# One maximum over two PSUM banks, and one sum for base and running counts, in an attention and mixture-of-experts kernel

## Chip, cores and metric

The kernel runs on one core of a Trainium2 chip. The metric is device microseconds of one execution, the median of three runs. Lower is better.

## The reference

Two stages, the second on the output of the first.

```python
def _attn_ref(q, k, v, omega):            # 8 x 8 heads, 576 tokens, head_dim 64, 128 features
    ...
    def phi(x):
        proj = np.einsum('bhsd,md->bhsm', x, omega)
        sq = np.sum(x * x, axis=-1, keepdims=True) / 2.0
        h = proj - sq
        h = h - np.max(h, axis=-1, keepdims=True)
        return np.exp(h) / np.sqrt(m)
    q_p, k_p = (phi(q_s), phi(k_s))
    kv = np.einsum('bhsm,bhsd->bhmd', k_p, v)
    z = np.sum(k_p, axis=2)
    num = np.einsum('bhsm,bhmd->bhsd', q_p, kv)
    den = np.einsum('bhsm,bhm->bhs', q_p, z)[..., None] + 1e-06
    return num / den
def _moe_ref(x, expert_emb, tau, w1, w2): # 4608 tokens of 512, 8 experts, hidden 1024
    ...                                   # logits of the normalised token and embeddings, one expert each
    out[mask] = gate_w[mask, None] * (np.maximum(x[mask] @ w1[e], 0.0) @ w2[e])
```

Only `proj` and the row maxima and exponentials of it matter here, and the running count of tokens per expert, from which each token's row in a sorted list follows.

## The kernel before

The first phase is attention and routing. It is a loop over steps `i` from 0 to 42. A step takes one tile of 128 tokens of the keys (`k`, tile `i`) and one tile of the queries (`q`, tile `iq = i - 6`); each tile comes in two halves `a` of four heads. So steps 0 to 5 have keys alone, steps 6 to 35 both, and steps 36 to 42 queries alone or nothing but their remainder. The instructions of all engines stand in the order in which the loop writes them out, and each engine takes its own in that order.

In a step with both, `proj` makes two pairs of projections, each four heads times 128 features in one PSUM bank: first `one`, that is `k` half 1 and `q` half 0 (tag `px`), then `two`, that is `k` half 0 and `q` half 1 (tag `py`). The order of the step is:

- TensorE: `proj(one)`; `qtr`, the transposes of the query features of the step before, into the two banks of `nub`; `proj(two)`; in some steps `kv_turn` (below); `num`, the numerators, into `nub`; in some steps `kv_logits`; `kvmm`, the products of key features and values.
- VectorE: maxima of `k` half 1 (L331); a copy of one bank of transposes (L405); maxima of `q` half 0, then of `q` half 1; in some steps `kv_turned` (L376); maxima of `k` half 0; the four operations of `num_out` (L429, L430, L432, L435), which divide the numerators; then what routing has due at the step's end.
- ScalarE: a copy of the other bank of transposes (L405); then the exponentials (`feats`, L338, four to a tile) of `k` half 1, `q` half 0, `q` half 1 and `k` half 0. An exponential takes its row maxima as bias, so it follows them.

Eight times, when a block of keys is complete, `kv_closed` copies its sums on ScalarE, GpSimd regroups them (L363), and in the step after that TensorE turns them (`kv_turn`, L372), VectorE copies the result out of PSUM (`kv_turned`, L376), and TensorE multiplies that copy with the embeddings (`kv_logits`, L384), which writes into one of the banks of `nub`. From step 6 on `kv_turned` stands in the list `then`, which the loop works off after the maxima of `q` half 1 and before those of `k` half 0; for the first block, in step 6, it stands in `after`, ahead of the maxima of `q` half 1. Of the eight steps six have both tiles: 10, 15, 19, 24, 28 and 33. Step 37 has queries alone.

Every three tiles `routed` works through one group: logits, the chosen expert, TensorE's counts `pr` in a bank of `nub` (L473, L475), and at the end of a later step the sum of counts and running counts `run` into `base` (L481) and the update of `run` (L482). GpSimd makes the row numbers from `base` (L484) and writes the tokens to their rows with an indirect DMA.

The second phase goes through 38 blocks of 128 sorted tokens of one expert each, with TensorE full of products with the experts' weights (L241). `bank` gives it PSUM banks by tag, `py` among them.

Of the kernel before, what the change touches and what calls it, by code (L numbers as in the profile page):

```python
# [11 lines left out]
F32 = mybir.dt.float32  # L12
# [5 lines left out]
ALU = mybir.AluOpType  # L18
AX = mybir.AxisListType
ET = mybir.EngineType  # L20
PSUM = bass.MemoryType.PSUM

P = 128
B, H, S, D, M = 8, 8, 576, 64, 128
E, F = 8, 1024
# [5 lines left out]
G = 3  # L31
REG = N + P
# [23 lines left out]
def attention_moe(ctx: ExitStack, tc: tile.TileContext, qT, kT, v1, omT, emb, tau, w1q, w2q, xs, out):  # L56
    nc = tc.nc
# [6 lines left out]
    ps = ctx.enter_context(tc.tile_pool(name="ps", bufs=1, space=PSUM))  # L64
# [214 lines left out]
    with ExitStack() as c1:  # L279
        p1 = c1.enter_context(tc.tile_pool(name="p1", bufs=2))  # L280
        small = c1.enter_context(tc.tile_pool(name="small", bufs=2))
        once = c1.enter_context(tc.tile_pool(name="once", bufs=1))
        nub = c1.enter_context(tc.tile_pool(name="psn", bufs=1, space=PSUM)).tile([P, 2, 512], F32, name="nub")
        nu = [nub[:, a, :] for a in range(2)]


        kva, kvs, st = {}, {}, {}
        sels = [once.tile([P, G + 1, E], BF16, name=f"sel{j}") for j in range(2)]
        for z in sels:
            nc.vector.memset(z, 0.0)  # L290
# [28 lines left out]


        def proj(*which):
            for w, i, a, tag in which:
                st["pj" + w, i, a] = ps.tile([P, 4, M], F32, name=f"pj{w}{i}_{a}", tag=tag, bufs=2)
            for c in range(4):
                for w, i, a, _ in which:
                    r = slice(a * D, (a + 1) * D)
                    nc.tensor.matmul(st["pj" + w, i, a][:, c, :], st[w, i][r, c, :], om[r, :], start=True, stop=True)  # L327

        def maxima(which, i, a, *_):
            nm = small.tile([P, 4], F32, name=f"nm{which}{i}_{a}", tag=f"nm{which}", bufs=4)  # L330
            nc.vector.tensor_reduce(nm, st["pj" + which, i, a], axis=AX.X, op=ALU.max, negate=True)  # L331
            st["nm" + which, i, a] = nm

        def feats(which, i, a, *_):
            pj, nm = st["pj" + which, i, a], st["nm" + which, i, a]
# [103 lines left out]
        def routed(g):  # L439

            eng = nc.gpsimd if g < NTILE // G - 1 else nc.vector

            def total(out, x, axes):

                if eng is nc.vector:
                    eng.tensor_reduce(out, x.rearrange(axes), axis=AX.X, op=ALU.add)
                    return
                for n in (4, 2, 1):
                    eng.tensor_tensor(x[:, :, 0:n] if n > 1 else out.unsqueeze(2), x[:, :, 0:n], x[:, :, n : 2 * n], op=ALU.add)

            bc = lambda a: a.unsqueeze(2).to_broadcast([P, G, E])
            ibc = lambda a: a.unsqueeze(1).to_broadcast([P, G, E])
            new = lambda n, shape, dt=F32: small.tile(shape, dt, name=f"{n}{g}", tag=n)
            raw = new("raw", [P, G, E])
            total(raw, st["lg", g], "p g h e -> p g e h")
            if eng is nc.gpsimd:
                yield
            mx = new("mx", [P, G])
            nc.vector.tensor_reduce(mx, raw, axis=AX.X, op=ALU.max)
            nc.vector.tensor_tensor(raw, raw, bc(mx), op=ALU.subtract)  # L460
            for j in range(G):
                nc.gpsimd.tensor_copy(st["xr", g * G + j][:, DM : DM + E], raw[:, j])
            yield
            sel = sels[g % 2][:, 0:G]
            nc.vector.scalar_tensor_tensor(sel, raw, 0.0, ibc(iotm), op0=ALU.is_ge, op1=ALU.mult)
            nc.vector.tensor_reduce(mx, sel, axis=AX.X, op=ALU.min)
            nc.vector.tensor_tensor(sel, ibc(iotm), bc(mx), op=ALU.is_equal)
            yield

            w = 512 - 8 * E  # L470
            pr = nu[1][:, w - (G + 1) * E : w].rearrange("p (j e) -> p j e", e=E)
            for o in range(0, P, 64):
                nc.tensor.matmul(pr[o : o + 64], tri[:, o : o + 64], sels[g % 2], start=True, stop=False)  # L473
                for j in range(G):
                    nc.tensor.matmul(  # L475
                        pr[o : o + 64, j + 1 :], one16[:, o : o + 64], sel[:, j : j + 1].to_broadcast([P, G - j, E]),
                        start=False, stop=j == G - 1,
                    )
            yield
            base = new("base", [P, G, E])  # L480
            nc.vector.tensor_tensor(base, pr[:, 0:G], run.unsqueeze(1).to_broadcast([P, G, E]), op=ALU.add)  # L481
            nc.vector.tensor_tensor(run, run, pr[:, G], op=ALU.add)  # L482
            yield
            eng.tensor_tensor(base, base, sel, op=ALU.mult)  # L484
            pos = new("pos", [P, G])
            total(pos, base, "p g e -> p g e")
            if g == GPICK:
                pick_first()

            for j in range(G):  # L490
                if j:
                    yield
                posi = new(f"posi{j}", [P, 1], I32)
                eng.tensor_copy(posi, pos[:, j : j + 1])
                xr = st["xr", g * G + j]
                w = nc.gpsimd.indirect_dma_start(
                    out=xs, out_offset=bass.IndirectOffsetOnAxis(ap=posi, axis=0),
                    in_=xr, in_offset=None, bounds_check=ROWS - 1, oob_is_err=False,
                )
                written(w)  # L500
            if g == GPICK:
                early.append(len(put))

        def pick_first():

            cnt = small.tile([P, E], F32, name="cnt0", tag="cnt")
            nc.vector.scalar_tensor_tensor(cnt, iote, -float(REG), run, op0=ALU.mult, op1=ALU.add)
            m = small.tile([P, 1], F32, name="m0", tag="m0")
            nc.vector.tensor_reduce(m, cnt, axis=AX.X, op=ALU.max)
            nc.vector.tensor_scalar(cnt, cnt, m, None, op0=ALU.is_ge)  # L510
            nc.vector.tensor_tensor(cnt, cnt, iotm, op=ALU.mult)
            nc.vector.tensor_reduce(m, cnt, axis=AX.X, op=ALU.min)
            at(ends, st["now"] + 1).append((first_known, m))
# [86 lines left out]
                loadk(i + 1, nc.sync)  # L600
            loadv(i)
        nc.vector.tensor_scalar(om, om, SCALE, None, op0=ALU.mult)  # L602
        warm = ps.tile([P, 512], F32, name="warm", tag="py", bufs=2)
        for j in range(WARM):
            nc.tensor.matmul(warm[:, j % 4 * P : (j % 4 + 1) * P], one16, one16, start=True, stop=True)

# [45 lines left out]
        for i in range(END + 1):  # L652
# [40 lines left out]
            if ts:  # L693
                num(iq - 1)
            go(after, i)
            for p in two[1:]:
                maxima(*p)
            u = (i - 1) % TPS
            sums = [(j, a, b) for j, b in ([(i - 2, 1)] if u == 5 else []) + [(i - 1, int(u > 4))] for a in range(2)] if ss else []
# [4 lines left out]
            go(then, i)  # L704
            for p in one[1:] if two else ():
                feats(*p)
            if one:
                for p in two[:1]:
                    maxima(*p)
            for x in sums:  # L710
                kvmm(*x)
            closed = ss and u in (4, 8)
# [33 lines left out]
            pass  # L746


        vt = nc.vector
        room, at0 = p1.tile([P, 4, P], F32, name="room", tag="kt").rearrange("p c m -> p (c m)"), [0]  # L750

        def t(n, w=E, dt=F32):
# [94 lines left out]
    ring = xgp + [p2.tile([P, PAY], F32, name=f"xg{t}", bufs=1) for t in range(NPRE + 1, 6)]  # L847

    def bank(name, tag, bufs=1):
        return ps.tile([P, 512], F32, name=name, tag=tag, bufs=bufs)  # L850

    def x_of(t, row):
        return xload(t, row, ring[t % len(ring) if t != "x" else 0])
# [330 lines left out]
```

## Time and profile before

| | |
|---|---|
| median of 3 runs | 664.64 us (664.15 to 665.15) |
| profiled execution | 658.2 us, its span from first to last instruction 656.4 us |
| first phase, steps with both tiles | 18.8 us to 184 us of the span |
| busy in the span | TensorE 631.7 us (96%), VectorE 497.3 us (76%), ScalarE 416.9 us (64%), GpSimd 328.5 us (50%) |
| granted TensorE clock | 0.996 of full speed |

The median lies 6.4 us above the profiled execution's own time, and that lies 1.8 us above its span. Busy shares are means over two phases with different limits, and matmuls overlap one another, so a busy TensorE is not a TensorE at its peak.

### The profile page before, as it was taken

The page shows a single profiled execution, that of the slowest core. Times are in us where ns is not written, and L with a number is a line of the kernel's source. Part 1 is how long each engine was busy: PE and PEld are TensorE (multiplying, and loading weights), DVE is VectorE, ACT ScalarE, POOL GpSimd, SP SyncE. Part 2 cuts the span into 40 slices and gives each one's busy share as a digit, 9 for nine tenths or more (in the row PEclk, how much of TensorE's full clock was granted, in tenths as well). Part 3 has the DMA queues.
Part 4 walks back from the last instruction along what each step waited for, and adds up shares of the span by engine and source line. Part 5 has one row for each costly group of instructions (what it writes and reads, how often), then busy time and mean ns, then how long its engine had stood idle before and what let it go on. Part 6 is the DMA issues. An engine that isn't in the chain of part 4 may idle for free. (4 is left out here: it accounts for less than half of the span.)

```text
span 656.4 us, 18641 instructions
## 1 busy us (share of the span) xinstructions
PE 631.7 (96%) x6339; PEld 532.1 (81%) x6340; DVE 497.3 (76%) x952; ACT 416.9 (64%) x1074; POOL 328.5 (50%) x414
## 2 busy tenths in 40 slices
PE   8999999998889999999999999999999999999993
PEld 7899999988877787888788888888888888888872
DVE  4789888899888736778787777777768787777771
ACT  6899899899877236645656565656555656565430
POOL 2013443448885425474556364646455554646352
PEclk9999999999999999999999999999999999999998
DMA  7547667678832388588898888978697878887710
GB/s 252 177 148 228 196 202 212 214 243 285 261 125 97 118 308 259 156 237 198 237 211 223 208 227 190 240 193 232 178 244 184 236 192 196 225 208 212 187 64 34
DMA packets 142362, 131.89 MB, mean 201 GB/s; under 512 B 106742, under 2 KB 106870, under 8 KB 142272
## 3 DMA queue, kind: packets, MB, share of 16 engines
q1 hardware_dynamic: 135808, 110.04, 62.8%
q0 software_dynamic: 6320, 20.38, 7.9%
q8 instruction: 57, 0.93, 0.6%
q10 hardware_dynamic: 144, 0.26, 0.2%
q14 instruction: 33, 0.27, 0.1%
HBM read 83.78 MB, written 21.97 MB: 161 GB/s over the span
## 5 line engine op out<-in xcount | busy, mean ns | idle before, releaser
L241 PE MATMUL nu<-w2h,hl 128*128 (+1 forms) x288 | 113.9, 395 | 0.4 <-DVE hl L948 0.4
L241 PE MATMUL nu<-w2h,hh 128*128 (+1 forms) x288 | 113.9, 396 | 0.0
L241 PE MATMUL nu<-w2l,hh 128*128 (+1 forms) x288 | 113.8, 395 | 0.0
L241 PE MATMUL pa<-w1h,xl 128*128 (+1 forms) x280 | 110.8, 396 | 0.4 <-DVE xl L947 0.4
L241 PE MATMUL pa<-w1h,xh 128*128 (+1 forms) x280 | 111.1, 397 | 0.0
L241 PE MATMUL pa<-w1l,xh 128*128 (+1 forms) x280 | 110.6, 395 | 0.0
L909 ACT ACTIVATE pl<-pa 128x512 uint16<-128x512 uint16 x68 | 40.1, 594 | 94.2 <-PE pa L241 56.0
L905 DVE TENSOR_REDUCE wd<-t 128x1024 uint16<-128x1024 uint16 x68 | 90.0, 1325 | 1.7 <-DMA t<-pl 1.7
L338 ACT ACTIVATE ftk<-pjk,nmk 128x128 f32<-128x128 f32 x288 | 84.9, 427 | 6.3 <-DVE nmk L331 6.0
L207 POOL TENSOR_TENSOR w1l<-raww,w1h 128x1024 f32 x34 | 83.7, 2461 | 7.4 <-DVE w1h L206 5.5
L905 DVE TENSOR_REDUCE pl<-pa 128x512 uint16<-128x512 uint16 x68 | 46.6, 688 | 51.6 <-ACT pl L909 51.5
L338 ACT ACTIVATE ftq<-pjq,nmq 128x128 f32<-128x128 f32 x288 | 80.0, 430 | 8.7 <-DVE nmq L331 7.8
L207 POOL TENSOR_TENSOR w2l<-raww,w2h 128x1024 f32 x34 | 82.1, 2415 | 2.4 <-issue 2.4
L327 PE MATMUL pjq<-om,qt 64*128 64x128 f32 x576 | 75.6, 283 | 1.1 <-ACT ftk L338 0.7
L327 PE MATMUL pjk<-om,kt 64*128 64x128 f32 x576 | 76.3, 285 | 0.3 <-DVE om L602 0.3
L944 ACT ACTIVATE hh<-wd 128x1024 fp32r<-128x1024 f32 x34 | 36.1, 1062 | 60.2 <-DVE wd L905 54.3
L327 PEld LDWEIGHTS pjk<-om,kt 64*128 64x128 f32 x576 | 65.1, 190 | 2.9 <-DVE om L602 0.6
L271 POOL DMA_INDIRECT y<-xgp x20 | 22.7, 1136 | 87.6 <-DVE xgp L248 84.1
L241 PEld LDWEIGHTS nu<-w2h,hl 128*128 128x128 f32 x288 | 54.0, 188 | 13.9 <-DVE hl L948 0.8
L327 PEld LDWEIGHTS pjq<-om,qt 64*128 64x128 f32 x576 | 63.9, 188 | 1.6 <-ACT ftk L338 0.9
L241 PEld LDWEIGHTS nu<-w2l,hh 128*128 128x128 f32 x288 | 54.1, 188 | 13.1
L241 PEld LDWEIGHTS nu<-w2h,hh 128*128 128x128 f32 x288 | 54.1, 188 | 13.0
(311 smaller groups left out, 1270.0 us busy)
## 6 DMA issues: line engine op xcount, KB each, us to landing
raww<-w1q SPq DMA_DIRECT2D x38, 512.0 KB, 3.9
raww<-w2q SPq DMA_DIRECT2D x38, 512.0 KB, 5.2
qt<-qT SPq DMA_DIRECT2D x36, 256.0 KB, 4.3
kt<-kT SPq DMA_DIRECT2D x35, 256.0 KB, 3.0
xgp<-xs SPq DMA_DIRECT2D x20, 260.5 KB, 2.8
xg<-xs SPq DMA_DIRECT2D x18, 260.5 KB, 2.9
rf<-w1q SPq DMA_DIRECT2D x4, 512.0 KB, 5.6
rf<-w2q SPq DMA_DIRECT2D x4, 512.0 KB
```

What stands on the lines that cost most here:

```text
L207: il = nc.gpsimd.tensor_tensor(at(l, dp), raw, at(h, dp).bitcast(F32), op=ALU.subtract)
L241: done.append(nc.tensor.matmul(dst, x[:, c * P : (c + 1) * P], ws.rearrange("p o f -> p (o f)"), start=(begin and i == 0 and k == 0), stop ...
L271: w = nc.gpsimd.indirect_dma_start(out=out, out_offset=bass.IndirectOffsetOnAxis(ap=xg[:, PAY - 1 : PAY].bitcast(I32), axis=0), in_=xg[:, ...
L327: nc.tensor.matmul(st["pj" + w, i, a][:, c, :], st[w, i][r, c, :], om[r, :], start=True, stop=True)
L338: nc.scalar.activation(ft[:, h, :], pj[:, h, :], AF.Exp, bias=nm[:, h : h + 1])
L905: nc.vector.tensor_reduce(to, src.unsqueeze(2), axis=AX.X, op=ALU.max)
L909: nc.scalar.activation(planes[1][:, o : o + 512], halved(src)[:, :, 1], AF.Copy)
L944: nc.scalar.activation(hh, wd[:, 0:F], AF.Relu)
```

## The change

In steps with both tiles the pair `two` goes into one tile of two PSUM banks, and one `tensor_reduce` of 1024 elements per partition (`maxima2`) takes the maxima of both halves, at the place where those of `q` half 1 stood. The maxima of `k` half 0 no longer have an instruction of their own behind `then`. The tag `py` moves from the pool `ps` with two buffers of a bank into the pool `psn` with one buffer of two banks; the warm-up tile goes to `px`; the second phase takes `py` from its own pool.

In `routed` one addition of 32 elements gives `base` and the new running counts together, where there were an addition of 24 elements and one of 8.

```diff
-        nub = c1.enter_context(tc.tile_pool(name="psn", bufs=1, space=PSUM)).tile([P, 2, 512], F32, name="nub")
+        psn = c1.enter_context(tc.tile_pool(name="psn", bufs=1, space=PSUM))
+        nub = psn.tile([P, 2, 512], F32, name="nub")
...
-        kva, kvs, st = {}, {}, {}
+        kva, kvs, st = {}, {}, {"run": run}
...
         def proj(*which):
-            for w, i, a, tag in which:
-                st["pj" + w, i, a] = ps.tile([P, 4, M], F32, name=f"pj{w}{i}_{a}", tag=tag, bufs=2)
+            if which and which[0][3] == "py":
+                two = psn.tile([P, 2, 4, M], F32, name=f"pj{which[0][1]}_2", tag="py")
+                for j, (w, i, a, _) in enumerate(which):
+                    st["pj" + w, i, a], st["two", w, i, a] = two[:, j], two
+            else:
+                for w, i, a, tag in which:
+                    st["pj" + w, i, a] = ps.tile([P, 4, M], F32, name=f"pj{w}{i}_{a}", tag=tag, bufs=2)
...
+        def maxima2(*two):
+            nm = small.tile([P, 2, 4], F32, name=f"nm2_{two[0][1]}", tag="nm2", bufs=3)
+            nc.vector.tensor_reduce(nm, st["two", *two[0][:3]], axis=AX.X, op=ALU.max, negate=True)
+            for j, p in enumerate(two):
+                st["nm" + p[0], p[1], p[2]] = nm[:, j]
...
-            base = new("base", [P, G, E])
-            nc.vector.tensor_tensor(base, pr[:, 0:G], run.unsqueeze(1).to_broadcast([P, G, E]), op=ALU.add)
-            nc.vector.tensor_tensor(run, run, pr[:, G], op=ALU.add)
+            sums = new("base", [P, G + 1, E])
+            nc.vector.tensor_tensor(sums, pr, st["run"].unsqueeze(1).to_broadcast([P, G + 1, E]), op=ALU.add)
+            st["run"], base = sums[:, G], sums[:, 0:G]
...
-        warm = ps.tile([P, 512], F32, name="warm", tag="py", bufs=2)
+        warm = ps.tile([P, 512], F32, name="warm", tag="px", bufs=2)
...
             go(after, i)
-            for p in two[1:]:
+            if one and two:
+                maxima2(*two)
+            for p in () if one else two[1:]:
                 maxima(*p)
...
             go(then, i)
             for p in one[1:] if two else ():
                 feats(*p)
-            if one:
-                for p in two[:1]:
-                    maxima(*p)
...
-        vt = nc.vector
+        vt, run = nc.vector, st["run"]
...
     def bank(name, tag, bufs=1):
-        return ps.tile([P, 512], F32, name=name, tag=tag, bufs=bufs)
+        return (pso if tag == "py" else ps).tile([P, 512], F32, name=name, tag=tag, bufs=bufs)
```

## Rows read from the trace of the kernel before

**Rows 1.** Windows: busy us of each engine (instructions), clock, DMA share, GB/s.

```profile
20.00:185.00 165.00, 157.68 (x3665) 149.12 (x3666) 145.06 (x358) 150.27 (x529) 74.53 (x199) 1.00 0.68 215
260.00:645.00 385.00, 383.86 (x1655) 308.12 (x1654) 291.78 (x417) 213.36 (x399) 207.26 (x104) 1.00 0.79 203
```

**Rows 2.** Waits, whole span: us in total, times, longest us.

```profile
ACT qp L405 <- PE nub L400: 11.0, 18, 1.8
...
ACT ftq L338 <- DVE nmq L331: 7.8, 7, 1.8
```

**Rows 3.** Line L331 by itself: duration ns min/median/max, first and last start.

```profile
L331 DVE TENSOR_REDUCE nmq<-pjq x72: 675/681/692, 20.7 to 211.0; 128x4 f32<-128x512 f32 x72
```

**Rows 4.** Line L905, a reduction of 1024 elements in the second phase.

```profile
L905 DVE TENSOR_REDUCE wd<-t x68: 1296/1322/1359, 257.0 to 622.8; 128x1024 uint16<-128x1024 uint16 x68
```

**Rows 5.** Timeline of VectorE, steps 10 and 11: start us, us, instruction [idle before].

```profile
41.98 1.28 DVE L331 TENSOR_REDUCE nmq<-pjq 128x4 f32<-128x512 f32 x2
...
44.89 0.17 DVE L429 TENSOR_SCALAR rr<-nub 128x8 f32<-128x8 f32 x1 [0.33 <-ACT ftq L338]
...
46.20 0.17 DVE L459 TENSOR_REDUCE mx<-raw 128x3 f32<-128x24 f32 x1
```

**Rows 6.** Timeline of VectorE, step 13.

```profile
57.98 1.28 DVE L331 TENSOR_REDUCE nmq<-pjq 128x4 f32<-128x512 f32 x2
```

**Rows 7.** Timeline of ScalarE, step 13.

```profile
58.78 2.21 ACT L338 ACTIVATE ftq<-pjq,nmq 128x128 f32<-128x128 f32 x8
60.78 1.24 ACT L338 ACTIVATE ftk<-pjk,nmk 128x128 f32<-128x128 f32 x4
```

**Rows 8.** Timeline of VectorE, step 15.

```profile
68.27 1.28 DVE L331 TENSOR_REDUCE nmq<-pjq 128x4 f32<-128x512 f32 x2
69.46 0.68 DVE L376 COPY xgp<-kvtr 128x512 f32<-128x512 f32 x1
```

**Rows 9.** Timeline of VectorE, steps 19, 24, 28 and 33, maxima of both `q` halves.

```profile
89.86 1.28 DVE L331 TENSOR_REDUCE nmq<-pjq 128x4 f32<-128x512 f32 x2
...
116.05 1.28 DVE L331 TENSOR_REDUCE nmq<-pjq 128x4 f32<-128x512 f32 x2
...
138.64 1.28 DVE L331 TENSOR_REDUCE nmq<-pjq 128x4 f32<-128x512 f32 x2
...
166.74 1.28 DVE L331 TENSOR_REDUCE nmq<-pjq 128x4 f32<-128x512 f32 x2
```

**Rows 10.** Timeline of TensorE, `kv_logits` in steps 10, 15, 19, 24, 28, 33.

```profile
44.18 0.59 PE L384 MATMUL nub<-enbd,xgp 128*64 128x16 f32 x16
...
70.20 0.65 PE L384 MATMUL nub<-enbd,xgp 128*64 128x16 f32 x16
...
92.10 0.59 PE L384 MATMUL nub<-enbd,xgp 128*64 128x16 f32 x16
...
118.22 0.59 PE L384 MATMUL nub<-enbd,xgp 128*64 128x16 f32 x16
...
140.65 0.59 PE L384 MATMUL nub<-enbd,xgp 128*64 128x16 f32 x16
...
168.67 0.65 PE L384 MATMUL nub<-enbd,xgp 128*64 128x16 f32 x16
```

**Rows 11.** Timeline of ScalarE, start of step 16.

```profile
74.38 0.60 ACT L405 ACTIVATE qp<-nub 128x512 f32<-128x512 f32 x1 [1.83 <-PE nub L400]
```

**Rows 12.** Timeline of VectorE, its last idle time ahead of steps 28 and 33.

```profile
121.84 0.69 DVE L331 TENSOR_REDUCE nmk<-pjk 128x4 f32<-128x512 f32 x1 [1.52 <-PE pjk L327]
...
154.25 0.69 DVE L331 TENSOR_REDUCE nmk<-pjk 128x4 f32<-128x512 f32 x1 [0.22 <-PE pjk L327]
```

**Rows 13.** Timeline of VectorE, end of step 41.

```profile
213.04 0.17 DVE L481 TENSOR_TENSOR base<-nub,run 128x24 f32<-128x24 f32 x1
213.25 0.16 DVE L482 TENSOR_TENSOR run<-run,nub 128x8 f32<-128x8 f32 x1
```

**Rows 14.** Timeline of TensorE, start of step 42.

```profile
213.56 0.71 PE L400 MATMUL nub<-ident,ftq 64*128 64x64 f32 x16 [0.21 <-DVE run L482]
```

More of the change, by code (lines that the diff above doesn't have):

```diff
@@ L506, in pick_first @@
             cnt = small.tile([P, E], F32, name="cnt0", tag="cnt")
-            nc.vector.scalar_tensor_tensor(cnt, iote, -float(REG), run, op0=ALU.mult, op1=ALU.add)
+            nc.vector.scalar_tensor_tensor(cnt, iote, -float(REG), st["run"], op0=ALU.mult, op1=ALU.add)
             m = small.tile([P, 1], F32, name="m0", tag="m0")
```

## The prediction

> **What bounds the kernel now.** I read the windows first. In the steps with both tiles TensorE is busy 157.7 of 165 us, ScalarE 150.3 and VectorE 145.1; in the second phase TensorE is busy 383.9 of 385 us [rows 1]. The second phase keeps its work, so only the first can move the time, and whatever the first gains or loses moves the second as a whole. In the first phase three engines are nearly full, so the share of busy time decides nothing. The waits say more: ScalarE's copy of transposes waited for TensorE in 18 of 36 steps, 11.0 us in all, while exponentials of queries waited for their maxima only 7 times [rows 2]. Then I read one step after another in the timelines of VectorE, ScalarE and TensorE, and asked for each maximum who needs it next and how long it has been ready.
>
> **What one maximum over two banks costs.** A maximum of 512 elements takes 0.68 us [rows 3], and two in a row take 1.28 us [rows 6], so the second starts 0.60 us after the first: the last 0.08 us overlap. The trace has no such operation with 1024 elements in PSUM. From below: a reduction of 24 elements takes 0.17 us [rows 5], so 488 elements more cost 0.51 us, 1.04 ns each, and 512 more cost 0.53: 1.21 us. From above: a reduction of 1024 elements of another type, out of SBUF, takes 1.32 us [rows 4]. I take 1.21, since it extends the same operation on the same memory. The operation behind it then starts 1.13 us after it; two single maxima need 1.20. So VectorE is spared 0.07 us in each of 30 steps, 2.1 us of its time in all.
>
> [...]
>
> **Who gets his maxima later.** Both halves' maxima now arrive when the long operation ends, 1.21 us after its start. For `k` half 0 that is no loss. For `q` half 1 it is 0.53 us later than before. In step 13 the long operation would start at 58.58, where the second of the pair at 57.98 did, and end at 59.79 [rows 6]. ScalarE does eight exponentials of queries from 58.78 on and turns to `k` half 0 at 60.78, 2.00 us for eight [rows 7], so it turns to `q` half 1 at 59.78. With some 0.06 us for the signal (the copy at 69.46 ends at 70.14, its user starts at 70.20 [rows 8, 10]) ScalarE is late by 0.07 us; with a long operation of 1.32 us, by 0.18. A delay of ScalarE counts where ScalarE is last. In half the steps its next copy waits for TensorE anyway [rows 2], and once ScalarE is late by 0.07, VectorE has that much of a start in the next step and the wait does not come again. I take 0.4 us, between nothing and 2.1 (30 x 0.07).
>
> **What stands behind the long operation.** VectorE's next instruction in six steps is `kv_turned`, the copy L376. It stood between the maxima of `q` half 1 and those of `k` half 0; now the maxima of `k` half 0 are done ahead of it, inside the long operation. TensorE's `kv_logits` waits for that copy, and behind it in TensorE's order stand `kvmm`, the next step's projections and transposes. Let T be the start of the pair of query maxima. Now the long one starts at T + 0.60, the copy at T + 1.73, the copy takes 0.68 [rows 8], and with 0.06 for the signal `kv_logits` starts at T + 2.47. Against the starts before [rows 5, 8, 9, 10]:
>
> - step 10: 44.45 against 44.18, 0.27 later
> - step 15: 70.74 against 70.20, 0.54
> - step 19: 92.33 against 92.10, 0.23
> - step 24: 118.52 against 118.22, 0.30
> - step 28: 141.11 against 140.65, 0.46
> - step 33: 169.21 against 168.67, 0.54
>
> That is 2.34 us. It lies on the path: TensorE has no wait between `kv_logits` and the next step's transposes, and ScalarE waits for these (1.83 us ahead of step 16 [rows 11]). VectorE too is held: `num_out` reads a bank that `kv_logits` writes, and starts only behind it, at 44.89 in step 10 [rows 5]. So the three engines move together, and no later stretch has a slack that all three share.
>
> From this goes what VectorE gains ahead of steps 28 and 33, where it runs without idle from 121.84 and from 154.25 on [rows 12]. Into step 28 it has three shortened steps and one shortened sum of counts (0.21, below): 0.42, which leaves 0.04 of the 0.46. Into step 33 two and one: 0.35, which leaves 0.19 of the 0.54. In the other four VectorE waited for TensorE at the step's start, and nothing is credited. Left: 0.27 + 0.54 + 0.23 + 0.30 + 0.04 + 0.19 = 1.57 us. With 1.32 us for the long operation and no credit it would be 2.34 + 6 x 0.11 = 3.0.
>
> **The sum of base and running counts.** L482 starts 0.21 us behind L481 [rows 13]; 32 elements in place of 24 cost 8 x 1.04 ns more. So the transposes that overwrite that bank may start some 0.19 us sooner. It counts where TensorE waits for L482, as in step 42 [rows 14]; earlier TensorE mostly has other work at that time. Three of the twelve groups reach this point where keys have run out; in two of them ScalarE also has weights or features of the first blocks to handle, so I take one, -0.2, between nothing and -0.6.
>
> **Edits at no cost.** The pair `two` now gets its banks when both earlier tiles are read. ScalarE reads `q` half 1 first and `k` half 0 last, and one of the two tiles waited for that last reader before. The warm-up tile in `px` is written and released by TensorE alone. The second phase's `py` banks are free long before they are needed, as their last readers are in the first phase. Each is hidden by TensorE's own order.
>
> **Sum.** 1.57 + 0.4 - 0.2 = 1.8 us more on the profiled span of 656.4 us, 658.2 us. I carry it to the median, which lies 6.4 us above the profiled execution's own 658.2 us, unchanged: 664.64 + 1.8 = 666.4 us, 0.27% slower. About 0.2%, 1.33 us, is what a measurement of this kernel can tell from no change.
>
> **Rivals.**
>
> - *Hidden.* The wait behind `kv_logits` is made up within a few steps, because VectorE is ahead at the end of such a step and ScalarE has its 11.0 us of idle time. Speaks for it: only two of the six (steps 15 and 33) have `kv_logits` hard on the copy now. Against: TensorE itself is what ScalarE waits for. Time: 664.6 us, from 663.9 with the sums of counts to 665.9. Chance 0.28.
> - *VectorE is the bound,* and each operation less shows. It decides from the point where VectorE, with no idle time, holds the other two in most steps, as it does ahead of steps 28 and 33. Then seven waits of ScalarE shorten by 0.07 and twelve sums by 0.21: -0.5 - 2.5 = -3.0, 661.6 us, if it also covers `kv_logits`. [...] Against: VectorE idles for TensorE at the start of many steps. Chance 0.08.
> - *The delay of `q` half 1 passes in every step,* ScalarE being as full as TensorE. 30 x 0.07 = 2.1 in place of 0.4: 3.5 more, 668.1 us. Against: the waits of ScalarE for TensorE absorb it. Chance 0.14.
>
> **How the numbers follow.** The forecast has 0.50. Its own bounds are 1.0 (no delay of ScalarE, all three tail gains) to 3.0 (a long operation near 1.32 us), 665.6 to 667.6; some 0.07 of it lies within 0.2%. So slower by over 0.2%: 0.43 + 0.14 = 0.57; within 0.2%: 0.28 + 0.07 = 0.35; faster: 0.08. The range leaves out the second rival and the upper end of the third: 664.0 to 668.4 us. Cases of both signs do not share it evenly; the forecast's own is 665.6 to 667.6.
>
> **What the changed profile would show.** One TENSOR_REDUCE of 128x1024 in 30 places at about 1.21 us. TensorE waiting for L376 ahead of L384 in steps 10, 15, 19, 24 with the amounts above, and the first phase ending about 1.8 us later. Exponentials of `q` half 1 with short waits for the long maximum. One addition at the place of L481 and no L482. The prediction is wrong if `kv_logits` starts no later relative to its step, if the phase's end does not move though it does, or if the long operation takes clearly other than 1.2 us.

## The result, and the profile after

The changed kernel takes 669.4 us (median of 6 runs, 668.3 to 670.4) against 664.4 us (6 runs, 662.7 to 665.8) for the kernel before: ratio 1.0075, 95% interval 1.0055 to 1.0094. It is slower, as predicted, but by 5.0 us in place of 1.8, and the time lies above the range, which ended at 668.4. A second timing later, beside other kernels, gave 1.0057 (1.0037 to 1.0077), 3.8 us. Together some 4.4 us.

One thing about the profiles comes first, since without it the two traces mislead. The profiled execution of before had taken 658.2 us, less than every timed run of that kernel (in 89 of them none took under 662.7). That of the changed kernel took 669.6, in the middle of its own runs. So the two spans differ by 11.3 us, the medians by 5.0. A second profile of the unchanged kernel (experiment 1) has a span of 661.9 us, and the comparisons below use that one.

The first lines of the page of the changed kernel:

```profile
span 667.7 us, 18587 instructions
## 1 busy us (share of the span) xinstructions
PE 636.0 (95%) x6339; PEld 531.8 (80%) x6340; DVE 491.5 (74%) x910; ACT 419.5 (63%) x1074; POOL 327.6 (49%) x414
```

The same line of the kernel before, in its first profile:

```profile
PE 631.7 (96%) x6339; PEld 532.1 (81%) x6340; DVE 497.3 (76%) x952; ACT 416.9 (64%) x1074; POOL 328.5 (50%) x414
```

VectorE does 42 instructions less (30 maxima and 12 sums) and is busy for 5.8 us less. So the change did take work off VectorE, and the kernel is longer all the same. The windows over the steps with both tiles (8 us wider than in [rows 1], with the same work) and over the same 385 us of the second phase:

```profile
22.00:195.00 173.00, 160.24 (x3663) 147.87 (x3665) 141.26 (x319) 152.09 (x528) 73.65 (x199) 1.00 0.64 204
271.30:656.30 385.00, 384.00 (x1657) 308.71 (x1656) 290.82 (x417) 213.49 (x399) 207.08 (x104) 1.00 0.79 203
```

The second phase is as full as before, 384.0 of 385 us of TensorE, so the time was lost in the first. The line of the long operation alone:

```profile
L342 DVE TENSOR_REDUCE nm<-pj x30: 1205/1214/1225, 25.3 to 191.2; 128x8 f32<-128x1024 f32 x30
```

It takes 1.21 us, as worked out. The waits of the changed kernel, us in total, times, longest:

```profile
ACT qp L417 <- PE nub L412: 13.1, 15, 2.3
...
ACT ftq L350 <- DVE nmq L337: 6.3, 5, 1.8
...
DVE nmk L337 <- ACT ftk L350: 4.1, 3, 1.4
```

The first two answer to [rows 2] and are not longer than in the second profile of before (15.3 and 7.9 us). In the last, VectorE waits for ScalarE, 3 times, ahead of a maximum. A maximum reads the projections that TensorE wrote; nothing of ScalarE's goes into it. The sum is no sign of the change, for the first profile of before has the same:

```profile
DVE nmk L331 <- ACT ftk L338: 4.1, 3, 1.5
```

The places are. In the kernel before, these waits stand ahead of the first maximum of a step (2, 4 and 7), which starts right after TensorE has written its projections. The three places in the changed kernel, in VectorE's timeline of steps 0 to 5:

```profile
7.29 0.68 DVE L337 TENSOR_REDUCE nmk<-pj 128x4 f32<-128x512 f32 x1
...
10.06 0.69 DVE L337 TENSOR_REDUCE nmk<-pj 128x4 f32<-128x512 f32 x1 [1.45 <-ACT ftk L350]
...
13.46 0.69 DVE L337 TENSOR_REDUCE nmk<-pj 128x4 f32<-128x512 f32 x1 [0.60 <-PE pj L333]
15.54 0.69 DVE L337 TENSOR_REDUCE nmk<-pj 128x4 f32<-128x512 f32 x1 [1.39 <-ACT ftk L350]
...
18.93 0.69 DVE L337 TENSOR_REDUCE nmk<-pj 128x4 f32<-128x512 f32 x1 [0.70 <-PE pj L333]
20.89 0.69 DVE L337 TENSOR_REDUCE nmk<-pj 128x4 f32<-128x512 f32 x1 [1.27 <-ACT ftk L350]
```

The tile name tells it: in steps 1, 3 and 5, which have keys alone, both halves carry the tag `py`, and since the change that is one tile `pj` of two banks. The maxima of half 0 are read from it, then ScalarE's exponentials of half 0 read it, and the maxima of half 1, though in the other bank, wait until these exponentials have ended (in step 1 at 8.83 + 1.20 = 10.03, then 10.06). ScalarE in step 1 of the changed kernel, and VectorE in step 3 of the second profile of before, which runs both maxima in one go:

```profile
8.83 1.20 ACT L350 ACTIVATE ftk<-pj,nmk 128x128 f32<-128x128 f32 x4
```

```profile
12.75 1.29 DVE L331 TENSOR_REDUCE nmk<-pjk 128x4 f32<-128x512 f32 x2 [0.59 <-PE pjk L327]
```

To see where the rest went, I took from each trace the end of the last exponential (L350) of a step, and from it the length of stretches of the first phase, in us:

```
steps                     0-5    5-7   7-10  10-12  12-18  18-20  20-27  27-30  30-35  35-41   0-41
before, first profile   11.76  10.65  14.86  10.86  31.88  11.10  37.44  16.68  29.88  29.14 204.25
before, second profile  11.74  10.64  14.83  10.87  34.29  12.19  39.57  17.59  29.72  30.35 211.79
changed                 13.78  10.78  14.91  11.34  34.43  12.65  39.49  18.16  30.18  30.84 216.55
changed, second profile 13.75  10.77  14.90  11.36  34.39  12.65  39.51  18.17  29.87  30.79 216.15
```

The two profiles of the changed kernel agree to 0.05 us in all stretches but one, so differences can be read. The two of before do not agree: the first lacks 0.9 to 2.4 us in each of five stretches, and the comparisons are with the second. Steps 0 to 5 lose 2.0 us. About 0.5 each is lost from 10 to 12, 18 to 20 and 27 to 30, stretches that follow a step of `kv_logits` (10, 19, 28) or hold it, and in the tail; next to nothing from 12 to 18 and 20 to 27, with steps 15 and 24. That is 4.4 to 4.8 us up to step 41. What lies behind it varies without order, 440.6 to 442.1 us in the last three.

### The profile page after: what moved, and what is told of

It is laid out like the page before. It is cut to its first block, busy times and chain, and to the rows that moved or that the text cites. A ratio compares the mean times of both kernels' runs of the same rounds, so it can differ in the third digit from the quotient of the medians.

```text
span 667.7 us, 18587 instructions
## 1 busy us (share of the span) xinstructions
PE 636.0 (95%) x6339; PEld 531.8 (80%) x6340; DVE 491.5 (74%) x910; ACT 419.5 (63%) x1074; POOL 327.6 (49%) x414
## 5 line engine op out<-in xcount | busy, mean ns | idle before, releaser
L241 PEld LDWEIGHTS pa<-w1h,xl 128*128 128x128 f32 x280 | 52.6, 188 | 12.9 <-DVE xl L229 0.2
L241 PEld LDWEIGHTS pa<-w1h,xh 128*128 128x128 f32 x280 | 52.6, 188 | 12.7 <-ACT sq L252 0.3
L241 PEld LDWEIGHTS pa<-w1l,xh 128*128 128x128 f32 x280 | 52.6, 188 | 12.4
L271 POOL DMA_INDIRECT y<-xg x18 | 21.0, 1167 | 84.4 <-DVE xg L248 84.1
L959 DVE SCALAR_TENSOR_TENSOR hl<-wd,hh 128x1024 fp32r<-128x1024 f32 x34 | 46.6, 1372 | 18.6 <-ACT hh L955 18.6
L429 PE MATMUL nub<-kvs,qp 128*64 128x73 f32 x1152 | 44.9, 229 | 8.1 <-DVE qp L417 5.7
```

Of the source, the lines that this page charges most:

```text
L241: done.append(nc.tensor.matmul(dst, x[:, c * P : (c + 1) * P], ws.rearrange("p o f -> p (o f)"), start=(begin and i == 0 and k == 0), stop ...
L271: w = nc.gpsimd.indirect_dma_start(out=out, out_offset=bass.IndirectOffsetOnAxis(ap=xg[:, PAY - 1 : PAY].bitcast(I32), axis=0), in_=xg[:, ...
L429: nc.tensor.matmul(pn[z * 64 : z * 64 + 64, a, h, :], st["qp", i, z][:, 4 * a + h, :], kvs[sb, int(b)][:, 4 * a + h, :], start=True, stop= ...
L959: nc.vector.scalar_tensor_tensor(hl, wd[:, 0:F], 0.0, hh.bitcast(F32), op0=ALU.max, op1=ALU.subtract)
```

## The experiments

**1. Before, a second time.** No edit.

> The kernel before, unchanged, for a second profile of it. Its one profiled execution took 658.2 us where its timed runs lie at 662.7 to 665.8; the changed kernel's profiled execution (669.6) lies among its own timed runs. In the changed kernel VectorE's first operation of num_out starts 0.6 to 1.3 us after num in steps 13, 16, 22 and 25, while TensorE pauses within kvmm; in the first profile of before it starts at once. Theory A: those pauses are not the change's; the quick execution lacked them, and a second profile lies near 664 us and shows them in the same steps. Theory B: the pauses come with the change; a second profile shows num_out at once behind num in those steps, and if it lies near 664 us the difference to 658.2 stands in other places.

It took 663.8 us, and Theory A holds. In step 13 of this trace VectorE, TensorE and GpSimd, in this order:

```profile
59.15 0.68 DVE L331 TENSOR_REDUCE nmk<-pjk 128x4 f32<-128x512 f32 x1
61.08 0.17 DVE L429 TENSOR_SCALAR rr<-nub 128x8 f32<-128x8 f32 x1 [1.25 <-PE nub L417]
```

```profile
58.28 1.25 PE L417 MATMUL nub<-kvs,qp 128*64 128x73 f32 x32
59.36 1.18 PE L353 MATMUL kva<-vt12v,ftk 128*64 128x65 f32 x29
60.97 0.34 PE L353 MATMUL kva<-vt12v,ftk 128*64 128x65 f32 x3 [0.42 <-issue]
```

```profile
59.61 0.99 POOL L496 DMA_INDIRECT xs<-xr,posi  x1 [0.28 <-POOL posi L494]
```

`num` is over at 59.53, but `num_out` starts at 61.08 and TensorE stops within `kvmm` until 60.97, 0.37 us after GpSimd has issued its indirect DMA. The same stands in steps 16, 22 and 25, and in the changed kernel, where in the four steps `num_out` starts 1.00 to 1.47 us after `num` ends and TensorE goes on 0.37 to 0.40 us after the issue. In the first profile of before `num_out` started at 59.78 in step 13. These pauses are not the change's.

**2. The fused sum alone.** In the kernel before:

```diff
+            sums = new("base", [P, G + 1, E])
+            nc.vector.tensor_tensor(sums, pr, st["run"].unsqueeze(1).to_broadcast([P, G + 1, E]), op=ALU.add)
+            st["run"], base = sums[:, G], sums[:, 0:G]
```

> The kernel before with the second part of the change alone: one sum of 32 elements for base and running counts, maxima as before. The prediction's term: -0.2 us (0 to -0.6), 664.2 us beside 664.4. Rival (VectorE the bound, every operation shows): 12 x 0.21 = -2.5 us, 661.9.

Ratio 0.9987 (0.9976 to 0.9998): 0.9 us quicker, 0.1 to 1.6, which excludes the 2.5 of the rival. Its profile, with 213.29 us for steps 0 to 41, shows no stretch in which it gains, so where the gain arises stays open.

**3. Banks independent.** In the changed kernel, for maxima and exponentials of the two halves of one tile:

```diff
                     st["pj" + w, i, a], st["two", w, i, a] = two[:, j], two
+                    st["mate", w, i, a] = which[1 - j][:3]
...
+        def apart_banks(kind, other, p, ins):
+            st[(kind,) + p] = ins
+            if ("mate",) + p in st and True:
+                for o in st.get((other,) + st[("mate",) + p], ()):
+                    for x in ins:
+                        tc.declare_no_dep(x.ins, o.ins.name, reason="another bank")
...
-            nc.vector.tensor_reduce(nm, st["pj" + which, i, a], axis=AX.X, op=ALU.max, negate=True)
+            m = nc.vector.tensor_reduce(nm, st["pj" + which, i, a], axis=AX.X, op=ALU.max, negate=True)
             st["nm" + which, i, a] = nm
+            apart_banks("max", "exp", (which, i, a), [m])
...
-            for h in range(4):
-                nc.scalar.activation(ft[:, h, :], pj[:, h, :], AF.Exp, bias=nm[:, h : h + 1])
+            es = [nc.scalar.activation(ft[:, h, :], pj[:, h, :], AF.Exp, bias=nm[:, h : h + 1]) for h in range(4)]
             st["f" + which, i, a] = ft
+            apart_banks("exp", "max", (which, i, a), es)
```

> The changed kernel, in which maxima and exponentials of different banks of the shared tile are declared independent in the steps with keys alone or queries alone (0 to 5, 36 to 41). Nothing else. Theory now: one tile for two halves makes VectorE wait for ScalarE in steps 1, 3 and 5 (gaps of 1.45, 1.39, 1.27 us ahead of the maxima of the second half; some 1.9 us at the end of step 5) and ScalarE for VectorE in steps 37, 39 and 41 (0.6 us each, 1.8); both go, 669.4 - 3.7 = 665.7 us. Rival (the prediction's own step, the shared tile costs nothing): 669.4, the same as the changed kernel.

Ratio 1.0014 (1.0001 to 1.0027), from 1.0057 to 1.0075 without: 3 to 4 us back by a statement that changes no instruction, only what waits for what.

**4. The six steps with `kv_logits` in the old order.** In the changed kernel, with the banks independent in these six steps:

```diff
-            if one and two:
+            alone = one and two and i in (10, 15, 19, 24, 28, 33)
+            if one and two and not alone:
                 maxima2(*two)
-            for p in () if one else two[1:]:
+            for p in () if one and not alone else two[1:]:
                 maxima(*p)
...
+            if alone:
+                maxima(*two[0])
```

> The changed kernel, in which steps 10, 15, 19, 24, 28 and 33, those with kv_turned and kv_logits, go back to two single maxima in the old order (queries' half 1, kv_turned, keys' half 0) on the shared tile, their banks declared independent there; the other 24 steps with both tiles keep the long operation. Theory of the prediction: kv_logits comes 0.23 to 0.54 us sooner in each, 1.6 us in all back (up to 3), 667.8 us (666.4). Rival: the loss lies elsewhere (ramp, tail, pauses in steps 13, 16, 22, 25) and TensorE's gain in the six steps is taken up within a step or two: 669.4, within 0.5.

Ratio 1.0050 (1.0032 to 1.0068), from 1.0057 and 1.0075. The stretch 10 to 12 is back at the level of before (10.93), so the delay behind the long operation is real in step 10. The profile lost 1.4 us in steps 5 to 7, which the edit does not touch: from 24 to 27 us TensorE's granted clock is 0.50, behind an idle time of 1.41 us. Five of the 11 timed runs have a mean clock of 0.992 or 0.993 and took 669.8 to 671.0 us; the other six, from 0.994 up, took 666.4 to 669.2. So the ratio is no clean measure of this edit.

**5. Both edits at once.**

> The changed kernel with both earlier edits at once: banks declared independent everywhere, and the old order with two single maxima in the six steps with kv_logits. The long operation stays in the other 24 steps, the sum of counts stays fused. Theory: the loss is made of two things that add, false waits inside the shared tile (ratio 1.0075 to 1.0014 with them gone) and the copy queued behind the long operation (1.0075 to 1.0050), so this kernel stands at 1.0075 - 0.0061 - 0.0025 = 0.9989, 0.7 us quicker than before. Rival: what TensorE gains in the six steps is taken up again once the ramp no longer is late; then it stays at 1.0014.

Ratio 1.0005 (0.9988 to 1.0022), 0.6 us below experiment 3 with an uncertainty of 1.4: neither theory is excluded. Of the stretches 10 to 12 is clearly shorter, 11.20 against 11.63, and 27 to 30 (17.71 against 18.35), which varies with a pause that is described below the table.

**6. No long operation at all,** the condition `alone = one and two`; shared tile and fused sum stay.

> The same with the old order and two single maxima in all 30 steps: no long operation is left, but the shared tile of two banks and the fused sum are. Theory A (the prediction's terms for the long operation alone, VectorE spared 0.07 us in 24 steps, half 1 of the queries 0.07 us late, net near nothing, and 0.5 us lost in step 6 where ScalarE waits): 0.4 us quicker than the kernel with the old order in six steps. Theory B (one operation less counts on VectorE): 24 x 0.07 = 1.7 us slower than it. Beside the kernel with the fused sum alone (0.9987) it shows what the shared tile itself costs: nothing, if its banks are independent.

Ratio 1.0000 (0.9986 to 1.0014), and 212.29 us for steps 0 to 41 against 212.13. The 24 long operations that experiment 5 has more are worth nothing that can be seen: this kernel is 0.3 us quicker, with an uncertainty of 1.5. That leaves Theory A and excludes the 1.7 us of Theory B. Beside experiment 2, which has no shared tile, it stands 0.9 us higher, with an uncertainty of some 1.2, so that the shared tile with independent banks costs nothing is not shown to better than that.

**7. `kv_turned` ahead of the long operation,** in the kernel of experiment 3:

```diff
-                at(then if i >= LAG else after, i + 1).append((kv_turned, sb, b))
+                at(after, i + 1).append((kv_turned, sb, b))
```

> The changed kernel with its banks declared independent, and kv_turned placed ahead of the long operation in the six steps, so that TensorE's kv_logits no longer waits for it. All 30 long operations stay. Theory A (TensorE's wait is what the six steps cost): 1.7 us quicker than the kernel with independent banks, 0.9989. Theory B (ScalarE is no less bound: the exponentials of query half 1 now wait for the copy and for the long operation, some 0.7 to 1.0 us in each of the six): nothing gained or slower than 1.0014.

Ratio 0.9986 (0.9972 to 1.0001): Theory A. VectorE, then ScalarE, in step 10 (this kernel's lines: copy L397, long operation L351, `rr` L450, exponentials L358):

```profile
43.56 0.69 DVE L397 COPY xgp<-kvtr 128x512 f32<-128x512 f32 x1 [0.50 <-PE kvtr L393]
44.17 1.22 DVE L351 TENSOR_REDUCE nm<-pj 128x8 f32<-128x1024 f32 x1
45.30 0.16 DVE L450 TENSOR_SCALAR rr<-nub 128x8 f32<-128x8 f32 x1
```

```profile
45.50 1.14 ACT L358 ACTIVATE ftq<-pj,nm 128x128 f32<-128x128 f32 x4 [0.88 <-DVE rr L450]
```

ScalarE does wait 0.88 us, as Theory B says, and the stretch 7 to 10 is 1.0 us longer (15.90). But 10 to 12 is 1.3 shorter than in experiment 3 (10.32 against 11.63): with `kv_logits` early TensorE gives the loss back in the next step, and 0.3 more. That much of Theory A is seen. Another 0.7 us of the difference lies in the stretch 27 to 30 (17.63 against 18.35), which has a long and a short form (below the table), so not all of the ratio need be the edit's.

**8. The third indirect DMA of a group one step later,** in the kernel of experiment 2:

```diff
-                for d, key in ((ends, i + 1), (mid, i + 2) if i >= NTILE else (ends, i + 1), (after, i + 2), (ends, i + 2), (ends, i + 2), (ends, i + 3), (ends, i + 4)):
+                for d, key in ((ends, i + 1), (mid, i + 2) if i >= NTILE else (ends, i + 1), (after, i + 2), (ends, i + 2), (ends, i + 2), (ends, i + 3), (mid, i + 5) if i + 5 < END else (ends, i + 4)):
```

> The kernel before with the fused sum, and one move: the third indirect DMA of each group stands in the middle of the next step instead of at the end of its own, so GpSimd no longer issues it right behind the second one, while num runs. Theory: the pause of TensorE and the late num_out in steps 13, 16, 19, 22, 25 (VectorE starts 1.0 to 1.5 us after num; TensorE resumes 0.4 us after the issue of that DMA ends) come with that DMA at that place; moved, num_out starts within 0.3 us of num in those steps and the time falls by up to the 5 us that the quick profile of before lacked, 659 to 663 us. Rival: the pause comes from something else that has the period of three steps; the time stays at 0.9987.

Ratio 0.9979 (0.9959 to 0.9999), runs from 659.3 to 666.9 us. The pauses in steps 13, 16, 22 and 25 are gone: 37.65 us for steps 20 to 27 against 39.57. But steps 30 to 35 take 33.27 against 29.72. VectorE and GpSimd in step 31:

```profile
162.95 2.98 DVE L467 TENSOR_TENSOR sel<-iotm,mx 128x24 bf16<-128x24 f32 x1
```

```profile
163.13 2.75 POOL L540 TENSOR_TENSOR w1l<-rf,w1h 128x256 fp32r<-128x256 f32 x4
```

An operation of 0.18 to 0.22 us takes 2.98 and ends with GpSimd's four subtractions. With the DMA at its old place these begin only behind that DMA (in the second profile of before at 168.32, with the operation at 166.68). TensorE stands idle meanwhile, for 3.45 us until 167.28, and from 167.5 to 170.5 us its granted clock is 0.50.

**9. Changed kernel again, and the ramp alone.** The second has independent banks in steps 0 to 5 only.

> The changed kernel, unchanged, beside the kernels of this group. Expected: ratio 1.0075 again (1.0055 to 1.0094); a second profile with waits of 1.3 to 1.5 us of VectorE ahead of the second maxima in steps 1, 3 and 5, as in the first. Rival: the ramp's loss belonged to that one execution.

> The changed kernel, in which maxima and exponentials of different banks of the shared tile are independent in steps 0 to 5 alone; the waits in steps 37, 39 and 41 stay. It divides the 4.1 us that independent banks gave back (1.0075 to 1.0014). Theory A, from the first profiles: the ramp is 1.9 us of it and the tail 1.8, ratio 1.0046. Theory B: ScalarE in the tail has its 1.1 to 1.8 us of idle time ahead of these exponentials, and the later ones absorb most of the delay; the profiles put the tail at 0.6 us, so the ramp gives nearly all, 1.0025 or less.

Ratios 1.0057 (1.0037 to 1.0077) and 1.0022 (1.0009 to 1.0035). The ramp gives back 2.3 us of time, and 11.79 against 13.75 us in steps 0 to 5; Theory B. Its VectorE no longer waits there:

```profile
7.66 0.68 DVE L345 TENSOR_REDUCE nmk<-pj 128x4 f32<-128x512 f32 x1
...
12.32 1.29 DVE L345 TENSOR_REDUCE nmk<-pj 128x4 f32<-128x512 f32 x2 [0.60 <-PE pj L334]
```

In the tail the order of the waits is the other way round: ScalarE's exponentials of half 0 wait for VectorE's maxima of half 1. ScalarE in step 37 of the changed kernel, then of experiment 3:

```profile
202.07 2.18 ACT L350 ACTIVATE ftq<-pj,nmq 128x128 f32<-128x128 f32 x8 [1.75 <-DVE nmq L337]
```

```profile
199.35 2.18 ACT L358 ACTIVATE ftq<-pj,nmq 128x128 f32<-128x128 f32 x8 [1.13 <-DVE nmq L345]
```

The wait is 0.6 us longer in steps 37 and 39 and 0.2 in step 41, but steps 38 and 40 are shorter in return, and steps 35 to 41 differ by 0.6 in all (30.80 against 30.21).

The stretches of all kernels so far, by their experiments:

```
steps                     0-5    5-7   7-10  10-12  12-18  18-20  20-27  27-30  30-35  35-41   0-41
2  fused sum alone      11.74  10.64  14.83  10.87  34.32  12.50  39.52  18.08  29.82  30.98 213.29
3  banks independent    11.77  10.79  14.91  11.63  34.12  12.15  39.57  18.35  29.93  30.21 213.43
4  old order in six     13.75  12.21  14.89  10.93  34.63  12.12  39.55  18.32  29.88  30.71 216.99
5  both                 11.75  10.77  14.90  11.20  34.14  12.15  39.48  17.71  29.83  30.19 212.13
6  old order in all     11.78  10.66  14.86  10.86  34.29  11.96  39.50  18.10  29.90  30.38 212.29
7  kv_turned ahead      11.77  10.78  15.90  10.32  34.02  12.02  39.53  17.63  29.91  30.22 212.11
8  DMA later            11.74  10.64  14.83  10.86  32.35  11.83  37.65  17.37  33.27  30.94 211.49
9  banks, ramp alone    11.79  10.77  14.89  11.64  34.13  12.64  39.54  17.69  30.11  30.80 214.00
```

Ramp and tail (0 to 5, 35 to 41) follow the edits, apart from the tails of experiments 2 and 8, which have no shared tile and yet take 30.9 to 31.0 us. These two differ from the others in the granted clock of TensorE. The pages of experiments 2, 4 and 8 show it, a digit for each 40th of the span:

```profile
PEclk9999999999998999999999999999999999999997
PEclk9899999999999999999999999999999999999997
PEclk9999999999898999999999999999999999999997
```

In no other profile does a digit ahead of the last fall below 9. In experiment 2 the clock is 0.50 from 202.5 to 205.5 us, in experiment 8 from 202 to 204.5, both in step 38, after TensorE had stood idle for 1.5 us. In the second profile of before it stands idle as long at the same place (1.44 us) and the clock stays up; what decides is not shown. So the tails of experiments 2 and 8 say nothing against the shared tile. From 30 to 35 experiment 8 has the lower clock beside VectorE's 2.98 us, and its loss of 3.4 us there is not divided between them.

Two other columns do not follow the edits: 18 to 20 takes 12.2 us in experiment 3, with the long operation in step 19, and 12.5 in experiment 2, without any; 27 to 30 takes 17.6 to 17.7 or 18.1 to 18.4, whatever the order in step 28. Both hold a pause of two lengths. Where the column is short, `num_out` of step 19 or 28 starts 1.2 us after `num` ends; where it is long, 1.9 to 2.0, and GpSimd has then begun the issue of its next indirect DMA ahead of `num_out`. The second profile of before has both short, experiment 2 and the changed kernel both long, experiment 3 the first short and the second long. So the losses of the changed kernel there can't be laid to `kv_turned`.

**10. The DMA moved in the first six groups alone** (`i + 5 < 32`), once in the kernel of experiment 7 and once in that of experiment 2.

> The changed kernel with independent banks and with kv_turned ahead of the long operation (0.9986 without more), and the third indirect DMA of the first six groups in the middle of the next step; the later groups keep their place, because there VectorE's L467 took 2.98 us beside GpSimd's subtraction when that DMA no longer stood ahead of it. Theory: the pauses in steps 13, 16, 19, 22 and 25 go and nothing takes their place: 3.5 us, 0.993. Rival: the time is taken up again in steps 28 to 37, where other waits stand: 0.9986.

> The kernel before with the fused sum alone, and the third indirect DMA of the first six groups moved in the same way. Theory: as far below the fused sum alone (0.9987) as the pauses are long, 0.993 to 0.994; beside the kernel with the long operation and the same move it shows what the long operation is worth at its best place: nothing that can be measured, by the prediction's terms (24 x 0.07 us saved, as much lost to the later half). Rival: the move gains nothing, 0.9987.

Ratios 0.9951 (0.9936 to 0.9966) and 0.9931 (0.9913 to 0.9949). The move gains 2.3 us in the first, 1.2 less than expected, and 3.7 in the second, each with an uncertainty of 1.4. The second is the quickest kernel of this study, 660.5 us (659.7 to 660.7), 4.6 us below before: two single maxima, the fused sum, and the moved DMA. The first, with the long operation at the best place found for it, is 1.4 us slower than that (660.2 to 662.7); by stretches up to step 41 it is 0.5 (208.16 against 207.62). VectorE and GpSimd of the second in step 13:

```profile
58.93 0.68 DVE L331 TENSOR_REDUCE nmk<-pjk 128x4 f32<-128x512 f32 x1
59.53 0.16 DVE L429 TENSOR_SCALAR rr<-nub 128x8 f32<-128x8 f32 x1
```

```profile
58.80 0.19 POOL L425 COPY xr<-ids 128x1 int32<-128x1 int32 x1
61.20 0.47 POOL L462 COPY xr<-raw 128x8 f32<-128x8 f32 x3 [2.21 <-DVE raw L460]
61.61 0.18 POOL L494 CAST posi<-pos 128x1 int32<-128x1 f32 x1
62.07 1.00 POOL L496 DMA_INDIRECT xs<-xr,posi  x1 [0.28 <-POOL posi L494]
```

GpSimd now waits for `raw` before it comes to that DMA, and `num_out` follows the maxima at once.

## Why the prediction was right in direction and too small

**The step that failed** is "Edits at no cost", in the words "The pair `two` now gets its banks when both earlier tiles are read ... Each is hidden by TensorE's own order." It asked when TensorE may write the shared tile, and not who reads its two halves at the same time. In steps with both tiles one operation reads both halves, and nothing is lost. But the tag `py` also serves steps 1, 3, 5 and 37, 39, 41, in which VectorE reads one half while ScalarE reads the other; as readers of one tile they are put in a row. Shown: with the banks independent the time falls from 1.0057 and 1.0075 to 1.0014, the ramp from 13.75 to 11.77 us, and the stretches 0 to 41 from 216.2 and 216.6 to 213.4. In the stretches that is 2.0 us in the ramp and 0.6 in the tail. The code of before had said so, in `qcopy`, where ScalarE and VectorE copy the two banks of `nub`:

```python
            if z == 0:
                tc.declare_no_dep(c.ins, st["cp", 1].ins.name, reason="another bank")
```

**The long operation** takes 1.21 us, as predicted, and by itself is worth nothing that can be measured: experiments 5 and 6 are equal.

**`kv_turned` behind the long operation** exists, and the start of `kv_logits` was worked out rightly: T + 2.47 us, and in the changed kernel it starts at T + 2.46 to 2.47 in all six steps. In the second profile of before it starts 0.27, 0.42, 0.24, 0.42, 0.48 and 0.53 us sooner after T, 2.36 in all where 2.34 were predicted. What of this reaches the time agrees with the 1.57 us predicted without being settled: by the ratios it is 0.5 to 1.7 us (experiment 4 against the two timings of the changed kernel), 0.6 (5 against 3) and 1.9 (7 against 3), each uncertain by some 1.4. By stretches it is shown for step 10 alone, 0.4 to 0.5 us where 0.27 was predicted; for steps 19, 28 and 33 it can't be told from the pauses. The waits in step 10 of the changed kernel, VectorE and then TensorE:

```profile
44.75 1.21 DVE L342 TENSOR_REDUCE nm<-pj 128x8 f32<-128x1024 f32 x1
45.88 0.68 DVE L388 COPY xgp<-kvtr 128x512 f32<-128x512 f32 x1
47.38 0.17 DVE L441 TENSOR_SCALAR rr<-nub 128x8 f32<-128x8 f32 x1 [0.82 <-PE nub L396]
```

```profile
46.61 0.64 PE L396 MATMUL nub<-enbd,xgp 128*64 128x16 f32 x16 [0.21 <-DVE xgp L388]
```

`num_out` waits 0.82 us for `kv_logits`, 0.33 before [rows 5]. Steps 15 and 24, with 0.54 and 0.30 predicted, lose next to nothing, and here the profile on which the sum was made had misled: in the second profile of before and in the changed kernel `num_out` of step 15 starts 0.42 us after the issue of GpSimd's indirect DMA ends (73.03 after 72.61, 75.74 after 75.32), and a delay of `kv_logits` is hidden under that. The credits for VectorE running without idle into steps 28 and 33 [rows 12] also rested on stretches without pauses.

**The later half of the queries**, 0.4 us predicted, shows in one place, step 6, where ScalarE has nothing else to do. ScalarE in the changed kernel, then in the second profile of before:

```profile
26.59 1.14 ACT L350 ACTIVATE ftq<-pj,nm 128x128 f32<-128x128 f32 x4 [1.63 <-PE kva L365]
```

```profile
24.09 1.14 ACT L338 ACTIVATE ftq<-pjq,nmq 128x128 f32<-128x128 f32 x4 [1.19 <-DVE nmq L331]
```

The wait is 0.44 us longer, the step 0.54 (from 5.46 to 6.00), and step 7 gives 0.40 of it back. In 23 of the other 29 steps the exponentials start 0.1 us behind the long operation, with at most 0.08 us of idle time ahead of them. In the stretches 5 to 7 and 7 to 10 the term comes to 0.2 us together. The rival that carried this delay through every step is refuted by the stretches 12 to 18 and 20 to 27: 0.07 in each step would be 0.4 and 0.5 us there, and they take 34.14 and 39.48 us in experiment 5, with the long operation in most of their steps, and 34.29 and 39.50 in experiment 6, without it.

**The fused sum** was to give 0.2 us and gave 0.9 (0.1 to 1.6); the operation takes 0.18 us:

```profile
L493 DVE TENSOR_TENSOR base<-nub,base x11: 179/180/191, 70.0 to 232.5; 128x32 f32<-128x32 f32 x11
```

**The sum, made up again,** by stretches, of 4.4 to 4.8 us up to step 41: 2.0 in the ramp and 0.5 in the tail for the shared tile, 0.2 from step 6 to step 10, 0.5 for the copy in step 10, 3.2 in all. The rest, 1.2 to 1.6 us, lies mostly in 18 to 20 (0.5) and 27 to 30 (0.6), where the changed kernel has the long pause (`num_out` 1.9 to 2.0 us after `num` in steps 19 and 28) and the second profile of before the short one (1.2). Experiment 2 has the long one in both steps without a long operation or a shared tile, so neither is needed for it; whether the change made it so stays open. By the ratios, all terms but the shared tile are what experiment 3 stands above before, 0.9 us (0.1 to 1.8); the 1.8 predicted for them lies at the upper edge, and the shared tile is what was missing.

**The other rivals.** The wait behind `kv_logits` is not made up in step 10; in steps 15 and 24 it is hidden, by a pause that the first profile did not have. VectorE is not the bound: it does 42 instructions less, and no kernel here gained by that beyond the fused sum.

## What to carry to other kernels

When two tiles become one, list for each step every engine that reads either half, in all steps that use the tag and not only in those for which the merge is meant: independence that came from separate tiles has to be declared again (without that the ramp took 2.0 us longer here). The operation that was made longer here was paid by what is queued behind it (0.4 to 0.5 us in step 10) and by who needs only its first half (a wait 0.44 us longer in step 6); the instructions saved, on an engine that is busy for 74% of the span, paid nothing that could be measured. And compare a profile's own time with the timed runs before its slacks are added up: the execution that was 1% quicker than all of these lacked waits that the others have. Read the granted clock as well before two profiles are set against each other stretch by stretch.

## What the runs showed of the hardware that was not expected

In these traces TensorE pauses, and VectorE starts late on what TensorE has finished, where GpSimd issues an indirect DMA while `num` ends (the ends of matmuls are modelled in a trace): in step 13 of the second profile of before `num_out` starts 1.5 us after `num`, and TensorE goes on 0.4 us after the issue. Moving that one DMA out of the way removed the pauses in steps 13, 16, 22 and 25 and gave 3.7 us (0.9987 to 0.9931, with an uncertainty of 1.4); those in steps 15, 19, 24, 28 and 33, at other issues, remain (1.2 to 1.5 us). That the pause goes with the DMA at this place is shown by that; why it does is not, and the place alone is not enough: in the first profile of before the same issue stood there (59.57 to 60.56, `num` ending at 59.65) without a pause.

Ahead of the end, the granted clock of TensorE fell to 0.50 in three of the 14 profiles, in experiments 2 and 4 once and in experiment 8 twice, each time after TensorE had stood idle for 1.4 to 3.5 us. Others of that length brought no fall: the changed kernel has one of 1.42 us at the place where experiment 4 has its 1.41.

In experiment 8 VectorE's L467 took 2.98 us beside GpSimd's subtractions; in the first profile of before its 12 executions take 0.18 to 0.22 us. It started at 162.95, while GpSimd was copying (162.74 to 163.17), and ended at 165.93, just behind four subtractions in a row, 163.13 to 165.88. The profile shows all of it as busy time; what held it is not shown.
